# A table-driven order for PE, tight exp bursts, and half of the output products moved from VectorE to ScalarE and GpSimd, in an induced-attention and gated-FFN kernel

## The chip, the cores and the metric

One core of one Trainium2 chip. The metric is the time of one execution in microseconds (us) on the device; lower is better. Profiles come from one profiled execution; times come from further executions. The engines are called PE (TensorE matmul), PEld (weight load), DVE (VectorE), ACT (ScalarE), POOL (GpSimd) and SP (SyncE, which issues nearly all of the DMAs here).

## The reference, cut to what matters

```python
# x: (4, 12416, 128); inducing: (32, 128); d_ff = 1536
def mab(q, kv):                       # attention, one head
    s = scale * (q @ kv.transpose(0, 2, 1))
    a = softmax(s)
    return a @ kv
h = mab(I, x)                         # 32 inducing points look at all of x
y = mab(x, h)                         # every token looks at the 32 results
g, v = y @ w_gate, y @ w_val          # then per token:
ffn  = (gelu(g) * v) @ w_out
out  = y + sigmoid(y @ w_res) * ffn
```

Since y = a @ h with only 32 rows of h, the kernel folds h into the weights: the gate and value layers become products of 64 rows (two copies of the 32 attention weights, for precision) with `hgv = h @ w`, and two of them sit side by side in PE's 128 rows.

## The kernel before: the parts that matter

A batch is 24 groups of 512 tokens and one of 128. A group of 512 has six slots of 1024 columns (two blocks of 128 hidden values for each of the 512 tokens). Per slot PE makes two pairs of gate and value halves, ACT takes the gelu of each gate half, DVE multiplies (`u`), and PE later multiplies `u` with `wO` into the one bank `f`. In parallel the kernel prepares h for the next batch (exps "a", accumulation, exps "b").

```python
    p_ge  = ...tile_pool(name="gelu", bufs=7)
    p_u   = ...tile_pool(name="up", bufs=6)
    p_fin = ...tile_pool(name="fin", bufs=2)          # th and at: two buffers each
    ps_g  = ...(bufs=3, PSUM); ps_v = ...(bufs=2); ps_f = ...(bufs=1)
    # ...
    def emit(gate, value):          # one pair of halves
        # ... PE: g and v matmuls, 64 rows each
        act.activation(ge_t[i][...], gb, AC.Gelu, ...)               # ACT, f32
        ve.tensor_tensor(u, ge_t.pop(i), v_t.pop(i), AL.mult)        # DVE, per slot

    class Last:                     # the output of a group
        def gate(self):             # "R": tanh of the residual gate
            self.th = p_fin.tile([P, TOK], FP32, name="th", tag="th")
            act.activation(self.th, self.mix(slice(0, 64)), AC.Tanh, bias=0.0, scale=0.5)
        def residual(self):         # "A": y itself, copied out of PSUM
            self.at = p_fin.tile([P, TOK], FP32, name="at", tag="at")
            act.activation(self.at, self.mix(slice(64, 128)), AC.Copy, ...)
        def end(self):              # the output product, the sum, the store
            ve.scalar_tensor_tensor(th, th, 1.0, f, AL.add, AL.mult)
            po.tensor_tensor(at, at, th, AL.add)
            sy.dma_start(out[...], at)

    for gi in range(ngrp):          # the order: f is the group's first slot
        at(f + 2, lg.gate, START)
        for i, n in enumerate((16, 8, 6, 9, 9)):
            at(f + 3 + i, lambda lg=lg, n=n: lg.mms(n), END)         # 48 f matmuls
        at(f + 5, lg.residual, START)
        at(f + 7, lg.end, LATE)
    # ... exps of a batch in a burst with single slots between, without gelus;
    #     before it the lead of gelu halves grows by one a group, up to LEAD = 10
```

The softmax here doesn't subtract the row's maximum and nothing guards it: scores larger than these inputs give would overflow.

Of the kernel before, what the change touches and what calls it, by code (L numbers as in the profile page):

```python
# [18 lines left out]
def kernel(  # L19
# [34 lines left out]
    Q = 4  # L54
# [16 lines left out]
    p_ge = ctx.enter_context(tc.tile_pool(name="gelu", bufs=7))  # L71
    p_u = ctx.enter_context(tc.tile_pool(name="up", bufs=6))
# [71 lines left out]
    def exps(kind, b, j0, j1, bank):  # L144

        t0 = j0 // WIDE * WIDE
        if j0 == t0:
            dt = FP16 if kind == "a" else FP32
            if min(WIDE, nblk - t0) > 2:
                e_t[kind] = p_sm.tile([P, 2 * TOK], dt, name="e" + kind, tag="e" + kind, bufs=3)  # L150
            else:
                e_t[kind] = p_sm.tile([P, 2 * M], dt, name="es" + kind, tag="es" + kind, bufs=1)
# [200 lines left out]
    class Last:  # L353
# [41 lines left out]
        def end(self):  # L395
            tw = self.tw
            ve.scalar_tensor_tensor(self.th[:, :tw], self.th[:, :tw], 1.0,  # L397
                                    self.ffn.rearrange("p k c -> p (k c)")[:, :tw],
                                    AL.add, AL.mult)
            po.tensor_tensor(self.at[:, :tw], self.at[:, :tw], self.th[:, :tw], AL.add)  # L400
            n0, w = blocks_of(self.k)
            r0 = self.b * N + n0 * P
            sy.dma_start(
                out[r0:r0 + w * P, :].rearrange("(p j) c -> p j c", j=w)[
                    :, self.j0:self.j0 + self.nk, :],
                self.at[:, :tw].rearrange("p (k c) -> p k c", c=P))
# [94 lines left out]

    flat = [(gi, si) for gi in range(ngrp) for si in range(len(groups[gi][4]))]
    nflat = len(flat)
    first = {}
    for i, (gi, si) in enumerate(flat):
        first.setdefault(gi, i)
    windows = {}
    bursts = {}
    LEAD = 10

    START, MIDDLE, END, LATE = range(4)

    def at(i, f, where=MIDDLE):
        windows.setdefault(i, []).append((where, f))

    for gi in range(ngrp):
        lg = Last(gi)
        f = first[gi]
        at(f + 2, lg.gate, START)
        if len(groups[gi][4]) == 6:  # L520
            for i, n in enumerate((16, 8, 6, 9, 9)):
                at(f + 3 + i, lambda lg=lg, n=n: lg.mms(n), END)
            at(f + 5, lg.residual, START)
            at(f + 7, lg.end, LATE)
        else:
            at(f + 3, lg.residual, START)
            at(f + 3, lambda lg=lg: lg.mms(len(lg.todo)), END)
            at(f + 3, lg.end, LATE)

    def plan(b):  # L530
# [3 lines left out]
        def bg(g, p, f, where=MIDDLE):  # L534
            at(i0 + 6 * g + p, f, where)

        def burst(i, kind):
            n = TOK // M
            bursts[i] = [(lambda j0=j0: exps(kind, nb, j0, min(j0 + n, nblk), bank_g()))
                         for j0 in range(0, nblk, n)]  # L540

        if b == 0:
            for i in range(1, ntile):
                bg(0, 1 + (9 * i) // 2, lambda i=i: weights_b(0, i))
        if nb < B:
            for k in range(ntile):
                i = (9 * k) // 2 + 1
                bg(1, i, lambda k=k: fetch(nb, k))
                bg(1, i + 5, lambda k=k: convert(nb, k, po, po))
                bg(1, i + 8, lambda k=k: turn(nb, k))  # L550

            burst(i0 + 6 * 12 + 3, "a")
            cuts = [0, 20, 40, 60, 80, nblk]
            for i, (j0, j1) in enumerate(zip(cuts, cuts[1:])):
                bg(13 + i, 2, lambda j0=j0, j1=j1: accumulate(nb, j0, j1, True, True))
            bg(18, 2, lambda: finish_h(nb))
            bg(19, 2, lambda: turn_h(nb))
            bg(19, 4, lambda: first_layer_t(nb, 0))
            bg(20, 2, lambda: first_layer_t(nb, 1))
            bg(20, 4, lambda: spread(nb, 0, PRE))  # L560
            bg(20, 5, lambda: spread(nb, PRE, FCH))
            burst(i0 + 6 * 20 + 3, "b")
            tb = i0 + 6 * 21 + 3
            for i in range(0, nblk, WIDE):
                n = i // WIDE
                at(tb + 4 * n, lambda i=i: sums_b(nb, i, po))
                at(tb + 4 * n + 4, lambda i=i: ones_b(nb, i), LATE)
            bg(22, 2, lambda: res_layer(nb))
            for i in range(ntile):
                j = 6 * 21 + 9 + (5 * i) // 2  # L570
                at(i0 + j, lambda i=i: weights_b(nb, i), END)

    for b in range(B):
        plan(b)

    ghalves = [(i, h) for i in range(nflat) for h in range(len(halves_of(i)))]
    base = [0]
    for i in range(nflat):
        base.append(base[-1] + len(halves_of(i)))
    sent = {"g": 0, "v": 0, "w": 0}  # L580

    def slot(want):

        i = sent["v"]
        while sent["g"] < base[i + 1]:
            emit(ghalves[sent["g"]], None)
            sent["g"] += 1
        for h in range(len(halves_of(i))):
            g = None
            if sent["g"] < min(want, len(ghalves)):  # L590
                g = ghalves[sent["g"]]
# [66 lines left out]
```

## Time and profile before

| | before |
|---|---|
| time, median | 853.86 us (852.45, 852.99, 854.73; a fourth run of 2239.26 lies far off and counts as slow) |
| span of the profiled run (which took 849.61 us), mean granted clock of TensorE | 847.8 us, 0.985 |
| busy: PE, DVE, ACT, POOL | 94%, 92%, 89%, 45% |
| idle of ACT behind a buffer of `th` or `at` | 1.3 us in all |
| from the end of batch 0 to those of 1, 2 and 3 | 202.2, 203.7, 185.7 us |

The end of a batch is the start of its last group's output product, read from the timeline. The lines of this profile stand in the prediction below: the page's busy row, groups of instructions (busy time and mean of one, then the engine's idle time before them and what ended it), and busy times by stretch.

### The profile page before, as it was taken

To read this page: it belongs to the slowest core of one execution; us is meant where nothing else is said; L and a number is where in the kernel's file an instruction comes from. 1 tells how busy PE (TensorE), PEld (TensorE's weight loads), DVE (VectorE), ACT (ScalarE), POOL (GpSimd) and SP (SyncE) were. 2 spreads that over 40 slices of the span, in tenths; PEclk is the share of its full clock that TensorE was granted. 3 is DMA by queue.
4 is the path that set the end of the run, shared out by engine and by line. 5 is a ranking of instruction groups with operands and counts; after the bars stand their busy time and mean duration, and the time that the engine had idled before them with its cause. 6 is when DMAs were issued, how large, how long until landed. Compare 5 with 4: busy or idle time off the path is not lost.

```text
span 847.8 us, 23930 instructions
## 1 busy us (share of the span) xinstructions
PE 794.0 (94%) x9586; PEld 476.9 (56%) x9586; DVE 780.2 (92%) x773; ACT 757.8 (89%) x1462; POOL 381.2 (45%) x376
## 2 busy tenths in 40 slices
PE   5789999999999999999999999999999999999997
PEld 4545555555555555555655555555565555555554
DVE  8679999899799999899889999979979999999997
ACT  5589998899999999898999999979899999999994
POOL 2438985111498776112278878411229721111112
PEclk9699999999999999999999999999999999999999
DMA  8327874001247787100117888201022621100111
GB/s 299 125 68 163 205 194 121 26 27 39 45 95 156 178 196 146 41 27 31 52 39 118 200 183 185 73 27 39 27 56 68 121 57 39 39 36 30 38 39 43
DMA packets 118992, 78.28 MB, mean 92 GB/s; under 512 B 97216, under 2 KB 99936, under 8 KB 118880
## 3 DMA queue, kind: packets, MB, share of 16 engines
q1 hardware_dynamic: 116592, 74.32, 35.7%
q10 hardware_dynamic: 2288, 2.43, 0.9%
q8 instruction: 75, 1.23, 0.6%
q14 instruction: 37, 0.30, 0.1%
HBM read 27.87 MB, written 25.43 MB: 63 GB/s over the span
## 4 chain that ended last, share of the span: by engine, by line
PE 74%; ACT 16%; DVE 4%; issue 4%; DMA 1%; POOL 1%; POOLq 0%; SPq 0%; DVEq 0%; ACTq 0%
PE f L373 32%; PE g L336 31%; ACT ge L342 14%; PE v L336 4%; PE g L381 3%; PE g L157 2%; DVE lo L121 2%; DVE hi L119 1%; PE g L175 1%; ACT th L387 1%; PE g L177 1%; DVE u L350 0%; DMA xf<-in_x_dram 0%; DVE th L397 0%; POOL a L283 0%
## 5 line engine op out<-in xcount | busy, mean ns | idle before, releaser
L350 DVE TENSOR_TENSOR u<-ge,v 128x1024 bf16<-128x1024 f32 x584 | 690.0, 1213 | 51.8 <-ACT ge L342 23.5
L342 ACT ACTIVATE ge<-g 128x512 f32<-128x512 f32 x1164 | 621.0, 604 | 45.2 <-PE v L336 41.1
L336 PE MATMUL g<-rt,hgv 64*128 64x512 f16 x1152 | 370.0, 380 | 30.1 <-ACT ge L342 18.3
L336 PE MATMUL v<-rt,hgv 64*128 64x512 f16 x1152 | 381.8, 384 | 0.4 <-DVE u L350 0.2
L373 PE MATMUL f<-wO,u 128*128 128x128 bf16 x4656 | 345.1, 221 | 1.1 <-DVE th L397 1.1
L373 PEld LDWEIGHTS <-u 128*128 128x128 bf16 x4656 | 262.7, 98 | 116.1 <-issue 104.8
L400 POOL TENSOR_TENSOR at<-at,th 128x512 f32<-128x512 f32 (+1 forms) x100 | 124.2, 1242 | 392.5 <-ACT ge L342 355.9
L336 PEld LDWEIGHTS <-hgv 64*128 64x128 bf16 x2400 | 111.5, 94 | 158.9 <-issue 98.7
L283 POOL TENSOR_TENSOR a<-eb,z 128x1024 f16<-128x1024 f32 (+1 forms) x49 | 91.1, 1863 | 7.6 <-DMA rt<-a 5.8
L381 PEld LDWEIGHTS <-rt 64*128 64x128 f16 x768 | 56.5, 94 | 51.0 <-issue 16.9
L121 POOL TENSOR_TENSOR lo<-xf,hi 128x1024 f16<-128x1024 f32 x36 | 76.9, 2135 | 0.3
L381 PE MATMUL g<-hra,rt 64*128 64x128 f16 x768 | 73.5, 215 | 0.6
L397 DVE SCALAR_TENSOR_TENSOR th<-th,f 128x512 f32<-128x512 f32 (+1 forms) x100 | 66.5, 665 | 1.0 <-PE f L373 1.0
L387 ACT ACTIVATE th<-g 128x512 f32<-128x512 f32 (+1 forms) x100 | 59.5, 595 | 3.6 <-PE g L381 2.2
L392 ACT ACTIVATE at<-g 128x512 f32<-128x512 f32 (+1 forms) x100 | 59.4, 594 | 3.0 <-PE g L381 3.0
L119 POOL CAST hi<-xf 128x1024 f16<-128x1024 f32 x36 | 37.3, 1036 | 31.2 <-DMA xf<-in_x_dram 17.7
L157 PEld LDWEIGHTS <-xt 128*128 128x128 f16 x768 | 23.2, 98 | 12.0 <-issue 11.7
L137 ACT ACTIVATE xt<-g 128x1024 f16<-128x1024 f16 x12 | 12.3, 1023 | 13.5 <-PE g L136 13.5
L136 PE MATMUL g<-identF,hi 128*128 128x128 f16 x96 | 10.7, 279 | 10.0 <-DVE hi L119 9.9
L261 POOL TENSOR_TENSOR zt<-zt 128x256 f32<-128x256 f32 (+5 forms) x36 | 15.0, 417 | 2.8
L136 PEld LDWEIGHTS <-hi 128*128 128x128 f16 x96 | 8.0, 126 | 12.3 <-DVE hi L119 12.3
L161 ACT ACTIVATE eb<-g 128x512 f32<-128x512 f32 x18 | 10.1, 595 | 5.0 <-PE g L157 4.5
(104 smaller groups left out, 248.6 us busy)
## 6 DMA issues: line engine op xcount, KB each, us to landing
out_dram<-at SPq DMA_DIRECT2D x96, 256.0 KB, 2.2
xf<-in_x_dram SPq DMA_DIRECT2D x42, 512.0 KB, 4.1
ge<-in_x_dram SPq DMA_DIRECT2D x6, 512.0 KB, 5.9
rt<-a SPq DMA_TRANSPOSE x49, 3.1
xt<-hi SPq DMA_TRANSPOSE x36, 3.3
ge<-in_moe_w_gate_dram ACTq DMA_DIRECT2D x1, 512.0 KB, 4.6
ge<-in_moe_w_val_dram ACTq DMA_DIRECT2D x1, 512.0 KB, 5.0
ge<-in_moe_w_out_dram ACTq DMA_DIRECT2D x1, 512.0 KB, 4.4
```

The costliest lines, as they stand in the source:

```text
L119: e_hi.tensor_copy(hi[:, :w, :], xf[:, :w, :])
L121: e_lo.tensor_tensor(lo[:, :w, :P], xf[:, :w, :], hi[:, :w, :], AL.subtract)
L283: po.tensor_tensor(a2[:, :n], ev[:, o:o + n, :].unsqueeze(2).to_broadcast([P, n, Q, M]), z[:, o:o + n].unsqueeze(2).unsqueeze(3).to_broadc ...
L336: pe.matmul(*t[n], start=True, stop=True)
L342: act.activation(ge_t[i][:, h * TOK:h * TOK + n], gb[:, :n], AC.Gelu, bias=0.0, scale=1.0)
L350: ve.tensor_tensor(u[:, :n], ge_t.pop(i)[:, :n], v_t.pop(i)[:, :n], AL.mult)
L373: pe.matmul(self.ffn[:, k, :], u_t[self.gi, si][:, o:o + P], wO[:, fc, :], start=first, stop=not self.todo, skip_group_check=True)
L381: pe.matmul(bank[:, k * P:(k + 1) * P], rt_t[self.b, self.k][rows, self.j0 + k, :], hra_t[self.b][rows, :], start=True, stop=True)
L387: act.activation(self.th[:, :self.tw], self.mix(slice(0, 64)), AC.Tanh, bias=0.0, scale=0.5)
L392: act.activation(self.at[:, :self.tw], self.mix(slice(64, 128)), AC.Copy, bias=0.0, scale=1.0)
L397: ve.scalar_tensor_tensor(self.th[:, :tw], self.th[:, :tw], 1.0, self.ffn.rearrange("p k c -> p (k c)")[:, :tw], AL.add, AL.mult)
L400: po.tensor_tensor(self.at[:, :tw], self.at[:, :tw], self.th[:, :tw], AL.add)
```

## The change

The intent was to fill the waits between three almost full engines: PE's order of a batch comes from a table found with a model of the queues, the exps come in short bursts, and DVE is relieved of half of its output products.

In the table a word is one slot. P is a slot with two gate halves, Q with one, V with none, G a lone gate half; a number is so many f matmuls; R is a tanh, A a residual copy, E one burst piece of exps, c, h, t, l, r, o are steps of preparing h. A star marks a group whose output leaves by ACT and Pool.

```diff
-    p_ge = ...(name="gelu", bufs=7)
-    p_u  = ...(name="up", bufs=6)
+    p_ge = ...(name="gelu", bufs=8)
+    p_u  = ...(name="up", bufs=8)
     # ... exps "a" and "b" now share one set of buffers
-        def end(self):
-            ve.scalar_tensor_tensor(th, th, 1.0, f, AL.add, AL.mult)
-            po.tensor_tensor(at, at, th, AL.add)
+        def end(self, on_act):
+            if on_act:
+                fe = p_fin.tile([P, TOK], FP32, name="fe", tag="fe", bufs=1)
+                act.activation(fe, f, AC.Copy, bias=0.0, scale=1.0)
+                po.tensor_tensor(th, th, fe, AL.mult)
+                po.tensor_tensor(at, at, fe, AL.add)
+            else:
+                ve.scalar_tensor_tensor(th, th, 1.0, f, AL.add, AL.mult)
+            po.tensor_tensor(at, at, th, AL.add)
     # ...
+    plan = [
+        "ARQ GG6PRG 6P P8G P5 3P6",
+        "PR8G P2 7P A9P P8 GP *",
+        "9P A11P A9P 11P G12P 5P *",
     # ... 9 rows
+        "11P 10P R13P Q14E EVEc AEEE9EQ",
     # ... 12 rows
+    ]
     # ... the same without E, c, h, t, l, r, o for the last batch
+    LEAD = 4
     # ... the scheduled offsets of gate, mms, residual, end and the bursts are
     #     removed; the loop reads the words and sends what they name
```

More of the change, by code (lines that the diff above doesn't have):

```diff
@@ L70 @@
     p_h = ctx.enter_context(tc.tile_pool(name="hpool", bufs=2))
-    p_ge = ctx.enter_context(tc.tile_pool(name="gelu", bufs=7))
-    p_u = ctx.enter_context(tc.tile_pool(name="up", bufs=6))
+    p_ge = ctx.enter_context(tc.tile_pool(name="gelu", bufs=8))
+    p_u = ctx.enter_context(tc.tile_pool(name="up", bufs=8))
     p_fin = ctx.enter_context(tc.tile_pool(name="fin", bufs=2))
@@ L147, in exps @@
         if j0 == t0:
-            dt = FP16 if kind == "a" else FP32
             if min(WIDE, nblk - t0) > 2:
-                e_t[kind] = p_sm.tile([P, 2 * TOK], dt, name="e" + kind, tag="e" + kind, bufs=3)
+                e_t[kind] = p_sm.tile([P, 2 * TOK], FP32, name="e", tag="e", bufs=3)
             else:
-                e_t[kind] = p_sm.tile([P, 2 * M], dt, name="es" + kind, tag="es" + kind, bufs=1)
+                e_t[kind] = p_sm.tile([P, 2 * M], FP32, name="es", tag="es", bufs=1)
+            if kind == "a":
+                e_t[kind] = e_t[kind].bitcast(FP16)
         e = e_t[kind]
@@ L393, in residual @@
                            bias=0.0, scale=1.0)
-        def end(self):
+        def end(self, on_act):
             tw = self.tw
-            ve.scalar_tensor_tensor(self.th[:, :tw], self.th[:, :tw], 1.0,
-                                    self.ffn.rearrange("p k c -> p (k c)")[:, :tw],
-                                    AL.add, AL.mult)
-            po.tensor_tensor(self.at[:, :tw], self.at[:, :tw], self.th[:, :tw], AL.add)
+            th, at = self.th[:, :tw], self.at[:, :tw]
+            f = self.ffn.rearrange("p k c -> p (k c)")[:, :tw]
+            if on_act:
+                fe = p_fin.tile([P, TOK], FP32, name="fe", tag="fe", bufs=1)[:, :tw]
+                act.activation(fe, f, AC.Copy, bias=0.0, scale=1.0)
[4 more added lines that the diff above has]
+            po.tensor_tensor(at, at, th, AL.add)
             n0, w = blocks_of(self.k)
@@ L405, in end @@
                     :, self.j0:self.j0 + self.nk, :],
-                self.at[:, :tw].rearrange("p (k c) -> p k c", c=P))
+                at.rearrange("p (k c) -> p k c", c=P))
     ident = konst.tile([P, P], FP32, name="ident")
@@ L495 @@
         pe.matmul(warm, wG[:, :P], wG[:, :TOK], start=True, stop=True)
+    plan = [
+        "ARQ GG6PRG 6P P8G P5 3P6",
+        "PR8G P2 7P A9P P8 GP *",
+        "9P A11P A9P 11P G12P 5P *",
+        "7RQ R5P 7P 12GP 11P 7P",
+        "6P 6AP 9PG 9P P10 AP *",
+        "10PG 6P 9PR 13Q P 10RP",
+        "7PR 6P6 P9 PA10 PA P3 *",
+        "6P8 PA6 3P 7P 4P 11QR *",
+        "2P12 RP7 2P5 P 8P12 AP15A *",
+        "P9 P 5P6 2P11 RP 11P",
+        "8P5 P9 AP1 14P P12 RP",
+        "9P 6P 9PR9 3P P5 9AP",
+        "11P 10P R13P Q14E EVEc AEEE9EQ",
+        "P15 10P GcP6R P8 P5 P6",
+        "2P A8P 5PG8G AP8 P5 P6 *",
+        "3P A9P 6P 7PR1 3cP cP5 *",
+        "P9R P9 P2 3P8 P12 AP *",
+        "7cP 4P10 PR10 P5 hP 12PR *",
+        "12P 9PA 8P 7P 12P t11Q",
+        "AP11 AP 11P l6QRR 9Q AP9G",
+        "P6 3P 3P 16EEVEEE2EE 9Q P",
+        "24P5 P4 2P A7PR 6P P10 *",
+        "RP 12PoA 10P3 P13 rP11 PR *",
+        "10P4 P10 PR9l 4P Q 16P",
+        "8AP9o PG15oo",
+    ]
+    plan_last = [
+        "ARQ GG6PRG 6P P8G P5 3P6",
+        "PR8G P2 7P A9P P8 GP *",
+        "9P A11P A9P 11P G12P 5P *",
+        "7RQ R5P 7P 12GP 11P 7P",
+        "6P 6AP 9PG 9P P10 AP *",
+        "10PG 6P 9PR 13Q P 10RP",
+        "7PR 6P6 P9 PA10 PA P3 *",
+        "6P8 PA6 3P 7P 4P 11QR *",
+        "2P12 RP7 2P5 P 8P12 AP15A *",
+        "P9 P 5P6 2P11 RP 11P",
+        "8P5 P9 AP1 14P P12 RP",
+        "9P 6P 9PR9 3P P5 9AP",
+        "11P 10P R13P Q14 V A9Q",
+        "P15 10P GP6R P8 P5 P6",
+        "2P A8P 5PG8G AP8 P5 P6 *",
+        "3P A9P 6P 7PR1 3P P5 *",
+        "P9R P9 P2 3P8 P12 AP *",
+        "7P 4P10 PR10 P5 P 12PR *",
+        "12P 9PA 8P 7P 12P 11Q",
+        "AP11 AP 11P 6QRR 9Q AP9G",
+        "P6 3P 3P 16V2 9Q P",
+        "24P5 P4 2P A7PR 6P P10 *",
+        "RP 12PA 10P3 P13 P11 PR *",
+        "10P4 P10 PR9 4P Q 16P",
+        "8AP9 PG15",
+    ]
+    old = {"f": 12, "R": 1, "A": 1}
+    LEAD = 4
     flat = [(gi, si) for gi in range(ngrp) for si in range(len(groups[gi][4]))]
@@ L506 @@
         first.setdefault(gi, i)
+    ghalves = [(i, h) for i in range(nflat) for h in range(len(halves_of(i)))]
     windows = {}
-    bursts = {}
-    LEAD = 10
-    START, MIDDLE, END, LATE = range(4)
-    def at(i, f, where=MIDDLE):
-        windows.setdefault(i, []).append((where, f))
-    for gi in range(ngrp):
-        lg = Last(gi)
-        f = first[gi]
-        at(f + 2, lg.gate, START)
-        if len(groups[gi][4]) == 6:
-            for i, n in enumerate((16, 8, 6, 9, 9)):
-                at(f + 3 + i, lambda lg=lg, n=n: lg.mms(n), END)
-            at(f + 5, lg.residual, START)
-            at(f + 7, lg.end, LATE)
-        else:
-            at(f + 3, lg.residual, START)
-            at(f + 3, lambda lg=lg: lg.mms(len(lg.todo)), END)
-            at(f + 3, lg.end, LATE)
@@ L530, in plan, with plan_rest, at @@
-    def plan(b):
+    def plan_rest(b):
         nb = b + 1
         i0 = first[b * gpb]
-        def bg(g, p, f, where=MIDDLE):
-            at(i0 + 6 * g + p, f, where)
-        def burst(i, kind):
-            n = TOK // M
-            bursts[i] = [(lambda j0=j0: exps(kind, nb, j0, min(j0 + n, nblk), bank_g()))
-                         for j0 in range(0, nblk, n)]
+        def at(i, f):
+            windows.setdefault(i0 + i, []).append(f)
         if b == 0:
             for i in range(1, ntile):
-                bg(0, 1 + (9 * i) // 2, lambda i=i: weights_b(0, i))
+                at(1 + (9 * i) // 2, lambda i=i: weights_b(0, i))
@@ L545, in plan @@
         if nb < B:
             for k in range(ntile):
-                i = (9 * k) // 2 + 1
-                bg(1, i, lambda k=k: fetch(nb, k))
-                bg(1, i + 5, lambda k=k: convert(nb, k, po, po))
-                bg(1, i + 8, lambda k=k: turn(nb, k))
-            burst(i0 + 6 * 12 + 3, "a")
-            cuts = [0, 20, 40, 60, 80, nblk]
-            for i, (j0, j1) in enumerate(zip(cuts, cuts[1:])):
-                bg(13 + i, 2, lambda j0=j0, j1=j1: accumulate(nb, j0, j1, True, True))
@@ L556, in plan @@
-            bg(18, 2, lambda: finish_h(nb))
-            bg(19, 2, lambda: turn_h(nb))
-            bg(19, 4, lambda: first_layer_t(nb, 0))
-            bg(20, 2, lambda: first_layer_t(nb, 1))
-            bg(20, 4, lambda: spread(nb, 0, PRE))
-            bg(20, 5, lambda: spread(nb, PRE, FCH))
-            burst(i0 + 6 * 20 + 3, "b")
-            tb = i0 + 6 * 21 + 3
-            for i in range(0, nblk, WIDE):
-                n = i // WIDE
-                at(tb + 4 * n, lambda i=i: sums_b(nb, i, po))
-                at(tb + 4 * n + 4, lambda i=i: ones_b(nb, i), LATE)
@@ L568, in plan @@
-            bg(22, 2, lambda: res_layer(nb))
+                i = (9 * k) // 2 + 7
+                at(i, lambda k=k: fetch(nb, k))
+                at(i + 5, lambda k=k: convert(nb, k, po, po))
+                at(i + 8, lambda k=k: turn(nb, k))
             for i in range(ntile):
-                j = 6 * 21 + 9 + (5 * i) // 2
-                at(i0 + j, lambda i=i: weights_b(nb, i), END)
+                at(6 * 21 + 9 + (5 * i) // 2, lambda i=i: due.append((nb, i)))
     for b in range(B):
-        plan(b)
@@ L576 @@
-    ghalves = [(i, h) for i in range(nflat) for h in range(len(halves_of(i)))]
-    base = [0]
-    for i in range(nflat):
-        base.append(base[-1] + len(halves_of(i)))
-    sent = {"g": 0, "v": 0, "w": 0}
-    def slot(want):
-        i = sent["v"]
-        while sent["g"] < base[i + 1]:
-            emit(ghalves[sent["g"]], None)
-            sent["g"] += 1
-        for h in range(len(halves_of(i))):
-            g = None
-            if sent["g"] < min(want, len(ghalves)):
-                g = ghalves[sent["g"]]
-                sent["g"] += 1
-            emit(g, (i, h))
-        sent["v"] += 1
@@ L596, in window_next @@
-    def window_next():
-        for _, f in sorted(windows.pop(sent["w"], []), key=lambda e: e[0]):
-            f()
-        sent["w"] += 1
-    lead = 2
-    while sent["w"] < nflat:
-        i = sent["w"]
-        assert i == sent["v"]
-        if i in bursts:
-            pieces = bursts.pop(i)
-            n = 0
-            while pieces:
-                if sent["g"] >= base[sent["v"] + 1]:
-                    slot(0)
-                    for f in [pieces.pop(0) for _ in range(min(2 - n % 2, len(pieces)))]:
-                        f()
-                    window_next()
-                    n += 1
-                else:
-                    pieces.pop(0)()
-            lead = 2
-            continue
-        if flat[i][1] == 0 and len(groups[flat[i][0]][4]) == 6:
-            lead = min(lead + 1, LEAD)
-        want = base[i + 1] + lead
-        slot(want)
-        window_next()
-        if sent["g"] < min(want, len(ghalves)):
-            emit(ghalves[sent["g"]], None)
-            sent["g"] += 1
@@ L627, with single, gate_half @@
-    assert not bursts
-    while windows:
-        window_next()
+        plan_rest(b)
+    due = []
+    inverted = {}
+    lasts = []
+    sent = {"g": 0, "v": 0, "R": 0, "A": 0}
+    last_of = [Last(gi) for gi in range(ngrp)]
+    on_act = [row.endswith("*") for b in range(B) for row in (plan if b < B - 1 else plan_last)]
+    def single():
+        g = gate_half()
+        if g is not None:
+            emit(g, None)
+    def gate_half():
+        if sent["g"] == len(ghalves):
+            return None
+        sent["g"] += 1
+        return ghalves[sent["g"] - 1]
@@ new lines, in products_out, with background, step @@
+    def products_out(n):
+        while n and lasts:
+            lg = lasts[0]
+            k = min(n, len(lg.todo))
+            lg.mms(k)
+            n -= k
+            if not lg.todo:
+                lasts.pop(0).end(on_act[lg.gi])
+    def background(nb):
+        n = TOK // M
+        cuts = [0, 20, 40, 60, 80, nblk]
+        todo = {"E": [], "l": [], "c": [], "o": []}
+        for kind in "ab":
+            for j0 in range(0, nblk, n):
+                todo["E"].append((kind, j0, min(j0 + n, nblk)))
+        todo["c"] = list(zip(cuts, cuts[1:]))
+        todo["o"] = list(range(0, nblk, WIDE))
+        todo["l"] = [0, 1]
+        def step(t):
+            if t == "E":
+                kind, j0, j1 = todo["E"].pop(0)
+                exps(kind, nb, j0, j1, bank_g())
+                if kind == "b" and (j1 == nblk or j1 % WIDE == 0):
+                    sums_b(nb, j0 // WIDE * WIDE, po)
+            elif t == "c":
+                accumulate(nb, *todo["c"].pop(0), True, True)
+            elif t == "h":
+                finish_h(nb)
+            elif t == "t":
+                turn_h(nb)
+            elif t == "l":
+                first_layer_t(nb, todo["l"].pop(0))
+                if not todo["l"]:
+                    spread(nb, 0, PRE)
+                    spread(nb, PRE, FCH)
+            elif t == "r":
+                res_layer(nb)
+            elif t == "o":
+                t0 = todo["o"].pop(0)
+                ones_b(nb, t0)
+                inverted[nb] = t0 + WIDE
+        return step
@@ new lines @@
+    for _ in range(2):
+        single()
+    for b in range(B):
+        step = background(b + 1)
+        words = [w for row in (plan if b < B - 1 else plan_last) for w in row.replace(" *", "").split()]
+        for w in words:
+            i = sent["v"]
+            if flat[i][1] == 0:
+                lasts.append(last_of[flat[i][0]])
+            todo = []
+            for t in w:
+                if t.isdigit() and todo and todo[-1].isdigit():
+                    todo[-1] += t
+                else:
+                    todo.append(t)
+            for t in todo:
+                if t in "PQV":
+                    for h in range(len(halves_of(i))):
+                        emit(gate_half() if t == "P" or (t == "Q" and h == 0) else None, (i, h))
+                    sent["v"] += 1
+                elif t == "G":
+                    single()
+                elif t.isdigit():
+                    n = int(t)
+                    if b == 0:
+                        n -= min(old["f"], n)
+                        old["f"] -= int(t) - n
+                    products_out(n)
+                elif t in "RA":
+                    if b == 0 and old[t]:
+                        old[t] -= 1
+                    else:
+                        lg = last_of[sent[t]]
+                        sent[t] += 1
+                        lg.gate() if t == "R" else lg.residual()
+                else:
+                    step(t)
+            if b == 0 and i in range(4, 4 + 6 * (LEAD - 2), 6):
+                single()
+            for f in windows.pop(i, []):
+                f()
+            while due and (due[0][0], blocks_of(due[0][1])[0]) < (due[0][0], inverted.get(due[0][0], 0)):
+                weights_b(*due.pop(0))
@@ L631 @@
+    while sent["A"] < ngrp:
+        if sent["R"] < ngrp and sent["R"] <= sent["A"]:
+            last_of[sent["R"]].gate()
+            sent["R"] += 1
+        last_of[sent["A"]].residual()
+        sent["A"] += 1
+    while lasts:
+        products_out(48)
 _INS = ['x', 'inducing', 'moe_w_gate', 'moe_w_val', 'moe_w_out', 'moe_w_res']
```

## The prediction

> **What bounds the kernel now.** I read the page's busy row first, then the busy times by stretch, then the starts of instructions in the timeline, because three engines are nearly full and the mean cannot say which one sets the pace.
>
> The page's busy row and its costliest groups (busy, mean ns of one | idle before it):
>
> ```profile
> PE 794.0 (94%) x9586; PEld 476.9 (56%) x9586; DVE 780.2 (92%) x773; ACT 757.8 (89%) x1462; POOL 381.2 (45%) x376
> ...
> L350 DVE TENSOR_TENSOR u<-ge,v 128x1024 bf16<-128x1024 f32 x584 | 690.0, 1213 | 51.8 <-ACT ge L342 23.5
> L342 ACT ACTIVATE ge<-g 128x512 f32<-128x512 f32 x1164 | 621.0, 604 | 45.2 <-PE v L336 41.1
> L336 PE MATMUL g<-rt,hgv 64*128 64x512 f16 x1152 | 370.0, 380 | 30.1 <-ACT ge L342 18.3
> ...
> L397 DVE SCALAR_TENSOR_TENSOR th<-th,f 128x512 f32<-128x512 f32 (+1 forms) x100 | 66.5, 665 | 1.0 <-PE f L373 1.0
> ```
>
> No engine has long holes. PE waits for ACT, ACT for PE, DVE for ACT: a ring of small waits. The durations overlap their neighbours, so I take start-to-start times as cost. The timeline late in the run (start, length, engine, instructions):
>
> ```profile
> 721.53 0.68 DVE L397 SCALAR_TENSOR_TENSOR th<-th,f 128x512 f32<-128x512 f32 x1
> ...
> 722.13 7.10 DVE L350 TENSOR_TENSOR u<-ge,v 128x1024 bf16<-128x1024 f32 x6
> ...
> 722.70 1.07 PE L373 MATMUL f<-wO,u 128*128 128x128 bf16 x16
> ...
> 723.70 0.39 PE L336 MATMUL v<-rt,hgv 64*128 64x512 f16 x1
> ...
> 723.92 0.38 PE L336 MATMUL v<-rt,hgv 64*128 64x512 f16 x1
> ...
> 724.23 0.62 PE L373 MATMUL f<-wO,u 128*128 128x128 bf16 x8
> ...
> 726.18 0.60 ACT L392 ACTIVATE at<-g 128x512 f32<-128x512 f32 x1
> ...
> 726.65 3.28 ACT L342 ACTIVATE ge<-g 128x512 f32<-128x512 f32 x6
> ...
> 729.15 0.68 DVE L397 SCALAR_TENSOR_TENSOR th<-th,f 128x512 f32<-128x512 f32 x1
> ...
> 729.75 7.10 DVE L350 TENSOR_TENSOR u<-ge,v 128x1024 bf16<-128x1024 f32 x6
> ```
>
> A group (512 tokens, six slots) takes 729.75 - 722.13 = 7.62 us here, and DVE is never idle: six u products and one output product (th). The output product holds DVE for 729.75 - 729.15 = 0.60. An ACT instruction on one bank holds ACT for 726.65 - 726.18 = 0.47. Over all starts in the trace the shortest repeating distances are: u 1.138, gelu 0.485 (mean of two kinds), tanh or copy 0.477, table load 1.294. On PE a gate/value pair costs 0.222, an f matmul 0.056, a mix matmul 0.055, and going from pairs to f and back adds about 0.09 + 0.095 (0.31 instead of 0.22, 0.151 instead of 0.056).
>
> The stretches (us, then busy us of PE, PEld, DVE, ACT, POOL) show that the limit changes:
>
> ```profile
> 60.00:140.00 80.00, 76.86 (x820) 44.86 (x819) 76.87 (x72) 75.38 (x149) 70.14 (x60) 1.00 0.77 179
> 150.00:205.00 55.00, 53.20 (x726) 31.83 (x723) 49.26 (x51) 49.44 (x97) 8.36 (x8) 1.00 0.09 31
> 300.00:340.00 40.00, 37.95 (x418) 21.95 (x415) 39.66 (x38) 37.96 (x75) 28.52 (x28) 1.00 0.75 161
> 720.00:835.00 115.00, 109.88 (x1219) 64.16 (x1215) 113.97 (x107) 109.09 (x213) 19.14 (x15) 1.00 0.10 36
> ```
>
> The steady stretches (rows 3 and 4) are DVE's, at 99%, 7.61 us per group. Row 1 is where ACT makes an extra gelu half per group to rebuild the lead of ten halves: 7.94. Row 2 has the accumulation of h in blocks of 40 matmuls: 8.43, PE. The last output product of each batch starts at 252.7, 454.9, 658.5 and 844.2, so batches 1 and 2 take 202.2 and 203.7, while batch 3, which prepares no successor, takes 185.7. **Preparing the next batch costs 16.5 to 18**, about half of it in two exp bursts. In the second of batch 0 ACT makes no gelu from 216.14 to 224.40, 8.3 us, and the group there takes 11.7.
>
> **What the Trainium skill says.** "TensorEngine Tiling (Array Packing)", Key Properties: changing the tiling mode drains the TensorE. The trace agrees: the 64-row pairs and the 128-row f matmuls pay the 0.185 a round trip above. "ScalarE: Activation LUTs", What ACT_TABLE_LOAD costs: 1283 ns plus a drain of some 1380. The load is 1283 here, but the next instruction starts 1.294 after it, so I count no drain. "PSUM — Partial Sum Buffer", Specifications: GpSimd cannot access PSUM. That is why ACT must copy f before Pool can use it. "SBUF — State Buffer", SBUF: two separate sides: Pool blocks a DVE instruction with two SBUF inputs. The u product takes one input from PSUM, and it lasts 1218 ns with Pool 88% busy (60 to 110) and with Pool 17% busy (720 to 835), so more Pool work should not slow it.
>
> **The change part by part.**
> (1) Twelve of 25 groups per batch, 48 in all, send the output product by ACT and Pool. DVE loses 48 x 0.598 = 28.7. ACT gains 48 copies x 0.477 = 22.9. Pool gains 2 x 48 tensor operations of about 1.23 each, 118.
> (2) The order of PE. The built programs have the same matmuls. The runs of f grow from 484 to 526: 42 x 0.185 = +7.8 on PE.
> (3) Exps in tight bursts: seven exps and two loads make 6 x 0.49 + 0.25 + 2 x 1.294 = 5.8 of ACT instead of the 8.3 seen. Table loads are not fewer. Six bursts x 2.5 = -15 at most.
> (4) Accumulation no longer sits as a block behind a slot, and the lead is 4 halves instead of 10, so no groups of thirteen gelu halves. Buffers for ge and u grow by one and two.
>
> Demand of the main loop (all after about 45 us), which now takes 798:
> - DVE before: 580 x 1.138 + 96 x 0.598 + 8 small = 725. After: 696.
> - ACT before: 1164 x 0.485 + 192 x 0.477 + 36 exps x 0.49 + 12 loads x 1.294 + 7 = 697. After: 720.
> - PE after: f 4656 x 0.056 = 261; pairs 1057 x 0.222 + 48 short = 237; lone gates and values 190 x 0.222 = 42; mixes 776 x 0.055 = 43; exps 582 x 0.025 = 15; accumulation 8; switches 526 x 0.185 + 5 = 102: 708. Before: 700.
>
> So the largest demand barely falls (725 to 720). **The move of products balances; the gain must come from the 73 us of holes that the order leaves.** A steady group after asks DVE for 6 x 1.138 + 0.3 = 7.13, ACT for 12 x 0.485 + 2.5 x 0.477 = 7.01, and PE for about 6.98 (708 less 34 for preparing, over 97). Before, DVE asked 7.43 and the group took 7.61, 2.4% more. I put 3% on 7.13, since three engines now lie close: 7.35. A batch is 24.25 groups: 178 instead of 185.7. Preparing asks ACT for some 13 (exps 6.4, loads 5.2, rest 1.3) and PE for about 12, partly side by side: I take 13, so batches 1 and 2 take 191 each.
>
> Batch 0 differs, because Pool also makes most of the weights of its own batch. From the built order, between its first and its last marked end in the first ten groups, Pool does 12 converts x 3.2 = 38.5, ten weights x 1.85 = 18.5 and 22 output operations x 1.23 = 27: 84, where ten groups at 7.35 are 74. Two buffers of th and of at can hide a lag of a group or so. I add 5: 196.
>
> Sum: 50 before the first batch's groups + 196 + 191 + 191 + 178 + 3.6 tail = 810, plus 6 (timed 854.73 against a span of 847.8) = 816. A table found in a model is not fully met on a chip; I add 4: **820 us**, 4% less.
>
> **Rivals.**
> - Pool takes DVE's place. One fe buffer and two of th and at tie ACT to Pool, and PE to ACT. For it: row 1 above, Pool at 88% already. Against: from 150 to 205 Pool is 15% busy, and batches 1 to 3 make fewer weights there. If it holds over a dozen groups in each of three batches, 8.2 per group: 840.
> - ACT becomes the bound. 720 of demand in a loop of 760 is 95%, and every late gate bank stops PE. Then groups stay at 7.5 to 7.6 and only the bursts and the rebuilding of the lead gain, 5 to 7 a batch: 832.
> - The short lead starves DVE in a burst: 4 halves are two u, 2.3 us against 5.8 without gelu. It is in the 13 above; if two bursts cost as now, 828.
> - The order is met exactly and PE's 708 is the limit: loop 740 to 745, so 800.
>
> **Range and chances.** The rivals span 800 to 840, so 800 to 842 holds 8 in 10. 2% faster is 837.6, above all rivals but one. Faster 0.78, same 0.18, slower 0.04.
>
> **What would show it.** DVE's th group x52 instead of x100, a new ACT group fe<-f x48 near 600 ns, three Pool operations per marked group. Ends of batches about 191 apart and the last 178; steady groups 7.2 to 7.45, none at 7.94 or 8.43; stretches without gelu near 6 instead of 8.3. Batch 0 slowest, Pool near full from 55 to 135. Wrong if ACT waits for Pool (fe, th) for tens of us, if DVE waits at bursts for more than 3 us each, or if u gets longer beside Pool.

## The result, and the profile after

The changed kernel takes **977.99 us** (974.61 to 979.63, four runs), against 853.86. The ratio is 1.1455, 95% interval 1.1409 to 1.1501: 14.6% slower. Ratios here and below are the mean time of one kernel's fast runs over that of the other's of the same rounds, so not quite the ratio of the medians quoted. The result is correct.

The page of the changed kernel, the busy row and the groups that answer to those of before:

```profile
PE 827.8 (85%) x9585; PEld 495.8 (51%) x9586; DVE 754.8 (77%) x725; ACT 773.7 (79%) x1510; POOL 500.3 (51%) x472
...
L351 DVE TENSOR_TENSOR u<-ge,v 128x1024 bf16<-128x1024 f32 x584 | 685.5, 1214 | 175.6 <-PE v L337 89.7
...
L337 PE MATMUL g<-rt,hgv 64*128 64x512 f16 x1152 | 392.1, 403 | 102.9 <-ACT at L393 66.2
...
L393 ACT ACTIVATE at<-g 128x512 f32<-128x512 f32 (+1 forms) x100 | 58.9, 589 | 104.0 <-DMA out_dram<-at 98.4
```

DVE has lost its 48 products (x725 instead of x773), as intended, but it now idles 175.6 us ahead of the u products instead of 51.8. The new name is in the last row: ACT idles 98.4 us ahead of the residual copy, and an output DMA ends it. PE's gate matmuls in turn wait 66.2 us for that copy. The list of waits of ACT (who waited, for whom: total us, times, longest):

```profile
ACT at L393 <- DMA out_dram<-at: 98.4, 28, 7.1
...
ACT th L388 <- POOL at L407: 19.8, 9, 6.5
```

In the kernel before there is no wait of the first kind, and one of the second:

```profile
ACT th L387 <- POOL at L400: 1.3, 1, 1.3
```

One such wait of the changed kernel (start, length, engine, instructions, idle before and what ended it), put together from the timelines of DVE, Pool, ACT, SP and ACT again:

```profile
239.38 0.69 DVE L406 SCALAR_TENSOR_TENSOR th<-th,f 128x512 f32<-128x512 f32 x1 [1.49 <-PE f L374]
...
237.63 1.28 POOL L259 TENSOR_TENSOR zt<-e 128x512 f32<-128x512 f32 x1 [10.83 <-ACT e L162]
...
249.07 1.26 POOL L407 TENSOR_TENSOR at<-at,th 128x512 f32<-128x512 f32 x1
...
240.92 4.51 ACT L343 ACTIVATE ge<-g 128x512 f32<-128x512 f32 x9
...
250.36 0.33 SPq L410 DMA_DIRECT2D out_dram<-at  x1
...
252.47 0.60 ACT L393 ACTIVATE at<-g 128x512 f32<-128x512 f32 x1 [7.04 <-DMA out_dram<-at]
```

Group 21's residual copy stands next in ACT's queue at 245.4. It needs the buffer of group 19, whose product was made at 239.4. But Pool first works off the sums of the exps "b", put into its queue earlier, adds group 19's residual only at 249.07, and SP sends the store at 250.36. ACT starts at 252.47, 7 us late, and the gelus behind it are late with it. Group 21 waits as long in batches 1 and 2 (7.1 us each). The stretch around it (us, busy us of PE, PEld, DVE, ACT, POOL, then the granted clock):

```profile
240.00:260.00 20.00, 12.68 (x124) 7.53 (x122) 11.53 (x12) 11.62 (x23) 10.27 (x20) 0.74 0.07 27
```

PE, DVE, ACT and Pool are busy only 51 to 63% of it, and the granted clock falls to 0.74; over the whole run it is 0.916 against 0.985. The Trainium skill, "TensorE: Matmul & The Clock Gate", HAM oscillation, warns of PE-idle gaps over some 3.4 us, after which the clock is throttled. The trace agrees in kind: after a 6.25 us idle of PE at 100.52, its gate matmuls last 0.58 to 0.61 us there, against 0.37 to 0.39 just before.

### The profile page after: what moved, and what is told of

The parts are those of the page before. It is cut to its first block, busy times and chain, and to the rows that moved or that the text cites. A ratio compares the mean times of both kernels' runs of the same rounds, so it can differ in the third digit from the quotient of the medians.

```text
span 975.1 us, 23933 instructions
## 1 busy us (share of the span) xinstructions
PE 827.8 (85%) x9585; PEld 495.8 (51%) x9586; DVE 754.8 (77%) x725; ACT 773.7 (79%) x1510; POOL 500.3 (51%) x472
## 5 line engine op out<-in xcount | busy, mean ns | idle before, releaser
L351 DVE TENSOR_TENSOR u<-ge,v 128x1024 bf16<-128x1024 f32 x584 | 685.5, 1214 | 175.6 <-PE v L337 89.7
L343 ACT ACTIVATE ge<-g 128x512 f32<-128x512 f32 x1164 | 607.6, 617 | 44.2 <-PE v L337 24.5
L337 PE MATMUL g<-rt,hgv 64*128 64x512 f16 x1152 | 392.1, 403 | 102.9 <-ACT at L393 66.2
L374 PE MATMUL f<-wO,u 128*128 128x128 bf16 x4656 | 370.8, 227 | 2.0 <-ACT fe L402 1.0
L374 PEld LDWEIGHTS <-u 128*128 128x128 bf16 x4656 | 279.2, 101 | 149.0 <-issue 138.1
L337 PEld LDWEIGHTS <-hgv 64*128 64x128 bf16 x2400 | 127.0, 95 | 230.7 <-issue 163.2
L393 ACT ACTIVATE at<-g 128x512 f32<-128x512 f32 (+1 forms) x100 | 58.9, 589 | 104.0 <-DMA out_dram<-at 98.4
L403 POOL TENSOR_TENSOR th<-th,fe 128x512 f32<-128x512 f32 x48 | 61.2, 1276 | 151.9 <-ACT fe L402 130.8
L284 POOL TENSOR_TENSOR a<-e,z 128x1024 f16<-128x1024 f32 (+1 forms) x49 | 90.9, 1863 | 11.3 <-DMA rt<-a 5.2
L388 ACT ACTIVATE th<-g 128x512 f32<-128x512 f32 (+1 forms) x100 | 59.5, 599 | 25.2 <-POOL at L407 19.8
L404 POOL TENSOR_TENSOR at<-at,fe 128x512 f32<-128x512 f32 x48 | 61.2, 1274 | 0.0
L406 DVE SCALAR_TENSOR_TENSOR th<-th,f 128x512 f32<-128x512 f32 (+1 forms) x52 | 33.9, 652 | 30.3 <-ACT th L388 22.3
L402 ACT ACTIVATE fe<-f 128x512 f32<-128x512 f32 x48 | 29.5, 615 | 5.3 <-PE f L374 4.6
L259 POOL TENSOR_TENSOR zt<-e 128x512 f32<-128x512 f32 x9 | 11.6, 1284 | 33.5 <-ACT e L162 33.0
```

The lines of the kernel that those rows point to most:

```text
L284: po.tensor_tensor(a2[:, :n], ev[:, o:o + n, :].unsqueeze(2).to_broadcast([P, n, Q, M]), z[:, o:o + n].unsqueeze(2).unsqueeze(3).to_broadc ...
L337: pe.matmul(*t[n], start=True, stop=True)
L343: act.activation(ge_t[i][:, h * TOK:h * TOK + n], gb[:, :n], AC.Gelu, bias=0.0, scale=1.0)
L351: ve.tensor_tensor(u[:, :n], ge_t.pop(i)[:, :n], v_t.pop(i)[:, :n], AL.mult)
L374: pe.matmul(self.ffn[:, k, :], u_t[self.gi, si][:, o:o + P], wO[:, fc, :], start=first, stop=not self.todo, skip_group_check=True)
L388: act.activation(self.th[:, :self.tw], self.mix(slice(0, 64)), AC.Tanh, bias=0.0, scale=0.5)
```

## The experiments

**Theory T (turnaround).** The table sends many R and A too soon. Counted from it, a residual copy comes 1 to 13 slots after the end of the group two before (1 in groups 9 and 20, 3 in group 19, 4 in groups 7, 10, 15 and 22), where the kernel before left 10 (5 to 9 next to the short group of 128; for `th` it is seven slots). ACT runs its queue in order, so it stands behind a buffer that Pool and the output DMA still hold. (The count is not the whole of it. Of the 28 waits, 12 are those of groups 9, 19 and 20 in each of the four batches, but group 22, four slots after, never waits and group 15 once, while group 21, five slots after, waits longest. What Pool has in its queue before that buffer counts too, as above.) **Theory P:** the three Pool operations of a marked group are too slow whatever the order. **Theory L:** the short lead of gelu halves starves DVE at the bursts.

### e1_defer: the same table, R and A held back

```diff
-                        lg.gate() if t == "R" else lg.residual()
+                        held.append((t, sent[t]))
+                        release()
     # ... release() sends what is held 7 slots after the end of the group two before,
     #     or when its own group is to end
```

> The changed kernel (978 us), its table and its routes kept; only a tanh or a residual copy is sent to the engines no sooner than seven slots after the group two before it has ended, so that its buffer of th or at is free when ACT comes to it. Theory T (turnaround: the table sends them one to five slots after that end, ACT stands in its queue behind a buffer that Pool and the output DMA still hold, and PE and DVE stand behind ACT): the 98 us of at <- DMA and 20 us of th <- Pool fall under 20 us together, time 850 to 890. Theory P (three Pool operations per marked group are too slow whatever the order): time stays above 940. Theory L (lead of four halves and tight bursts starve DVE): time stays above 930, waits of ACT gone.

889.8 us (ratio 1.0479). The waits of ACT for `at` fell to 27.7 us, those for `th` to 3.5:

```profile
ACT at L393 <- DMA out_dram<-at: 27.7, 13, 4.2
```

The waits are not all gone: together they are 31 us, where T expected under 20, and the time is at the upper end of what T gave. Nine of the 13 waits for `at` (15 us) come behind a marked group. The other four (12.5 us) come behind an unmarked one, and three of them are group 21 again, behind Pool's sums of the exps. Sending R and A later, with nothing else changed, takes back some 88 of the 124 us lost.

### e2_fin3: a third buffer of th and of at

```diff
-            self.th = p_fin.tile([P, TOK], FP32, name="th", tag="th")
+            self.th = p_fin.tile([P, TOK], FP32, name="th", tag="th", bufs=3)
-            self.at = p_fin.tile([P, TOK], FP32, name="at", tag="at")
+            self.at = p_fin.tile([P, TOK], FP32, name="at", tag="at", bufs=3)
-    p_ge = ...(name="gelu", bufs=8)
+    p_ge = ...(name="gelu", bufs=7)     # for the room
```

> The changed kernel with three buffers of th and of at instead of two (one buffer of ge given up for the room, 7 instead of 8). Order and routes the same. Theory T: the waits of ACT for the output DMA and for Pool nearly vanish, time 840 to 890. Theory P: Pool's chain of three operations still delays, time above 940. Theory L: above 930.

856.39 us (ratio 1.0086): nearly all of the loss is gone with one more buffer each, as T expected. The granted clock is 0.971, and ACT's wait for the output DMA is down from 98.4 us to:

```profile
ACT at L393 <- DMA out_dram<-at: 8.2, 5, 1.9
```

### e9_ge7 and e10_at3: which of the three edits did it

```diff
 e9_ge7:   ge bufs 8 -> 7, th and at stay at two
 e10_at3:  ge bufs 8 -> 7, at gets three buffers, th stays at two
```

> Control for the run with three buffers of th and at (856), which also gave up one of the eight ge buffers: the changed kernel with seven ge buffers and nothing else. If the third th and at buffers made the 122 us of difference: no better than the changed kernel, 975 to 990. If the eighth ge buffer did harm: clearly below 970.

> The changed kernel with seven ge buffers and a third buffer of at alone; th keeps two. The waits of ACT were 98 us for at (released by the output DMA) and 20 us for th (released by Pool). If the residual's buffer is the one: the 98 us go and the time is 860 to 895, with the waits for th at 20 us or somewhat more. If th matters as much: over 910.

e9_ge7 took 979.74 us, the same as the changed kernel: the ge buffer has no part in it. e10_at3 took 875.75 us. So the third `at` is worth 979.7 - 875.8 = 104 us, and the third `th`, from there to 856.4, another 19. With `at` mended, ACT stands behind `th` more than it did (32.0 us instead of 19.8):

```profile
ACT th L388 <- POOL at L407: 32.0, 19, 6.0
```

### e3_no_act: every product back on DVE, two buffers

```diff
-                lasts.pop(0).end(on_act[lg.gi])
+                lasts.pop(0).end(False)
```

> The changed kernel with the order kept, but every output product on DVE again, none by ACT and Pool. Theory P: the whole loss goes, 840 to 870. Theory T: the release of th and at comes some 2.5 us earlier in marked groups, the waits in unmarked groups stay (A one slot after the end), so a third to a half of the loss goes: 900 to 940. Theory L: 960 or more.

924.93 us (ratio 1.0893), inside what T gave and outside P and L. A product on DVE frees `at` after one Pool operation instead of three, which shortens the waits (67.3 us of ACT for the DMA instead of 98.4) but doesn't remove them: the order is enough to make them.

### e4_before_early: the same fault put into the kernel before

```diff
-            at(f + 5, lg.residual, START)
+            at(max(f - 4, 0), lg.residual, LATE if gi > 1 else START)
```

> The kernel before (854 us) with one thing changed: the residual copy is sent one slot after the group two before it has ended, nine slots sooner than it was. If theory T is right this alone breaks the good kernel: ACT waits 1.3 (Pool) + 2 (DMA) + issue, some 2 to 3 us per group, for the output DMA, 100 to 250 us of waits in all and a time of 950 to 1050, with a lower granted clock. If ACT's waits are hidden by the lead of ten gelu halves, it stays within 3% of 854.

**1162.19 us** (ratio 1.3687). One line of order, with no other engine, buffer or product changed, costs 313 us (the kernel before took 849.22). The list of waits has the same pair as the changed kernel, in 90 of 100 groups:

```profile
ACT at L392 <- DMA out_dram<-at: 277.4, 90, 5.1
...
PE g L336 <- ACT at L392: 171.8, 86, 4.2
```

I expected 100 to 250 us of waits and 950 to 1050. The waits came out a little above that (277.4 us), and their price well above: each wait of 3.1 us on ACT costs the loop some 3.5 us, the lower clock (0.906) included. The lead of up to ten gelu halves did not hide it.

### e5_fin3_no_act, e6_fin3_late, e11_fin3_last: what the move to ACT and Pool is worth

With three buffers, so that the turnaround no longer hides it, the marks (all marked groups in e2_fin3) were removed altogether, in the first thirteen groups of batches 0 to 2, and everywhere but in the last batch.

```diff
 e5_fin3_no_act:  end(False) for all groups
 e6_fin3_late:    marked only where b == B - 1 or the row is past the 13th
 e11_fin3_last:   marked only where b == B - 1
```

> Three buffers of th and at (which gave 856), and in addition every output product on DVE again. Tells what the move to ACT and Pool is worth once the buffers do not stop ACT. If Pool, overloaded by the move in the first half of batches 0 to 2, is what keeps the 856 from the 820 predicted: it falls, to 835 to 848. If the move balances the engines as predicted: DVE gets 29 us more and the time rises to 865 to 880.

> Three buffers of th and at; products leave by ACT and Pool only where Pool has room (the second half of batches 0 to 2, and the whole last batch). If Pool's load in the first half is the rest of the loss: batch 0 falls from 210 to about 200 and batches 1 and 2 by some 4 each, 836 to 845. If the rest lies in the order itself (bursts, short lead, groups over 8 us without background): within 5 us of 856.

> Three buffers of th and at, and products by ACT and Pool in the last batch only, where Pool has nothing else to do. Put together from the batches of the two runs with three buffers: batches 0 to 2 as with all products on DVE (start to 654.3), the last as with the move (183.1): a span of 841 and a time of 840 to 844, the best of both.

| kernel | time | ratio | from first product to end of batch 0 | batch 1 | batch 2 | batch 3 |
|---|---|---|---|---|---|---|
| before | 853.9 | 1 | 195.4 | 202.2 | 203.7 | 185.7 |
| after | 978.0 | 1.1455 | 233.4 | 237.3 | 238.9 | 204.7 |
| e2_fin3, all marks | 856.4 | 1.0086 | 201.1 | 206.6 | 201.7 | 183.1 |
| e5_fin3_no_act, no marks | 848.0 | 0.9935 | 193.5 | 200.2 | 199.9 | 188.6 |
| e6_fin3_late | 845.8 | 0.9912 | 194.7 | 201.3 | 203.0 | 183.1 |
| e11_fin3_last | **843.7** | **0.9885** | 195.5 | 200.3 | 199.9 | 182.9 |

The move gains 188.6 - 183.1 = 5.5 us in the last batch, where Pool has nothing else to do. It costs 7.6 us in batch 0, where Pool makes the weights and converts the next batch: ACT stands there once for 7.3 us (at 122.4 in e2_fin3), until Pool has read the one buffer of `fe`. In batches 1 and 2 it costs 6.4 and 1.8 us. e5_fin3_no_act (848.0) is at the upper edge of what Pool's load gave and far from the 865 to 880 of a move that balances; e6_fin3_late (845.8) missed its 836 to 845 by under 1 us, e11_fin3_last met its own. The version with marks in the last batch only, put together from these columns before it ran, is the best correct kernel: 1.15% faster than the kernel before (95% interval 0.7 to 1.6%).

### e12_lead6: a longer lead

```diff
-    LEAD = 4
+    LEAD = 6            # on e11_fin3_last
```

> The kernel of e11_fin3_last with two more gelu halves made ahead of use during the first batch and kept from there on (lead six instead of four). Theory L, that the short lead starves DVE at the exp bursts: DVE's idle time in the 16 us from a burst's start falls from 3.2 and 2.8 to under 2 and the time by 4 to 10 us. If PE's order and its waits are the limit instead: within 3 us of that kernel.

925.68 us, 82 us more than e11_fin3_last, which neither theory expected. DVE's idle time in the 16 us from a burst's start did not fall (3.23 and 2.79 us in e11_fin3_last, 4.01 and 2.78 here). In the kernel before, with its long lead, it was 3.5 and 4.1, so the short lead starves DVE at the bursts no more than the old order did. The list of waits names the cause of the longer time (the same wait is 5.3 us in e11_fin3_last):

```profile
ACT ge L343 <- DVE u L351: 74.8, 123, 1.9
```

It is the same fault with another buffer: two more gelu halves need one more ge tile, there are only seven, and ACT stands in its queue until DVE has read one. So this run says nothing against a longer lead with enough buffers; that stays open. It is one more case of an order and a number of buffers that don't fit.

### e7_before_act, e8_before_act_late: the move alone, in the old order

```diff
 e7: end(on_act) as in the change, for groups 1, 2, 4, 6, 7, 8, 14 to 17, 21, 22 of every batch
 e8: the same for groups 12, 14, 16, 18 of batches 0 to 2, and for thirteen of the last batch
```

> The kernel before (849 to 854) with its own order and its two buffers, only the same twelve of 25 groups' products sent by ACT and Pool. There ACT comes to a buffer some 10 us after Pool has done with it, so theory T expects no waits of ACT for at or th beyond 10 us in all. If the move alone is worth anything: the steady DVE-bound groups fall from 7.61 to about 7.3 in the last batch, but Pool is overloaded in the first half of batch 0: 842 to 856. If Pool's three operations harm by themselves: over 865.

> The kernel before with products sent by ACT and Pool only where Pool has room: four groups in the second half of batches 0 to 2, and thirteen of the last batch. The last batch should go from 185.7 to 178 to 181, the others stay: 840 to 848, the best so far if the move is worth anything. If PE, not DVE, sets the pace of the steady groups, no change: within 2 us of the kernel before.

891.29 us (1.0441) and 871.03 us (1.02, 95% interval 1.015 to 1.025): both slower. e7 lies in the branch that Pool's three operations do harm by themselves (over 865), e8 outside both of its own. T's part held roughly: the waits for `th` and `at` in e7 are 11.0 and 2.4 us, a little over the 10 expected, and 4.5 more are for `fe`. What failed is the gain itself. In the last batch of e8, marked and unmarked groups alternate, and two take 7.14 + 8.41 = 15.55 us instead of 2 x 7.61 = 15.22. The timeline there shows why:

```profile
796.38 0.60 ACT L401 ACTIVATE fe<-f 128x512 f32<-128x512 f32 x1
...
796.86 1.11 ACT L342 ACTIVATE ge<-g 128x512 f32<-128x512 f32 x2
...
797.53 0.37 PE L336 MATMUL g<-rt,hgv 64*128 64x512 f16 x1 [0.57 <-ACT ge L342]
...
797.82 0.64 ACT L387 ACTIVATE th<-g 128x512 f32<-128x512 f32 x1
...
798.52 1.22 DVE L350 TENSOR_TENSOR u<-ge,v 128x1024 bf16<-128x1024 f32 x1 [0.43 <-ACT th L387]
```

The copy of f holds ACT for half a microsecond just where PE needs a gelu bank back. PE's wait there grows from 0.25 to 0.57 us, and the DVE that has been relieved waits. This fits the last batch of e8, which takes 3.9 us more than before, but not all of the loss: of the 23 us between the two profiled runs 12.8 lie in batch 0, where ACT waits twice for `th`, 7.4 us in all, before any marked group has ended. Why it waits there is not known. Nor is Pool's share in the loss of e7 parted from that of the copy.

### e13_before_no_th, e14_fin3_no_th: is DVE the bound at all?

The product (tanh + 1) x f is left out. Their outputs are wrong, which doesn't matter for the times. (The comparison with the reference still passed both, as the term is small for these inputs; the kernels are not valid all the same.)

```diff
-            ve.scalar_tensor_tensor(th, th, 1.0, f, AL.add, AL.mult)
+            # nothing; at + th goes out
```

> WRONG RESULTS ON PURPOSE. The kernel before with its output product (tanh + 1) x f left out: DVE loses 100 instructions, 0.598 us each, 60 us of demand, and no engine gets anything in exchange. The prediction took the steady groups (7.61 us, DVE 99% busy) as set by DVE. If they are: these groups fall to about 7.0 and the time to 815 to 830. If the order of PE and ACT sets them and DVE only fills the same time: groups stay within 0.15 of 7.61 and the time within 12 us of the kernel before.

> WRONG RESULTS ON PURPOSE. The same product left out of the kernel with the new order, three buffers of th and at and all products on DVE (848). If DVE bounds it: 800 to 820. If PE's order and its waits for gelu banks bound it: 835 or more, which leaves the move of products to ACT and Pool nothing to win in either order.

In the old order, 60 us of DVE work taken away for nothing gave 847.11 us, ratio 0.9934 (0.9900 to 0.9969). The steady groups still take 7.61 us. The same stretch of the kernel before and of e13_before_no_th (first PE, PEld, DVE, ACT, POOL), one fence each:

```profile
720.00:810.00 90.00, 85.91 (x949) 49.94 (x946) 89.25 (x84) 85.27 (x167) 15.31 (x12) 1.00 0.10 37
```

```profile
720.00:810.00 90.00, 85.91 (x950) 49.97 (x947) 83.89 (x71) 85.28 (x166) 15.36 (x12) 1.00 0.10 37
```

PE's 85.91 and ACT's 85.27 don't move; only DVE's 89.25 becomes 83.89. **The engine that was busy 99% did not set the pace.** What is left to set it is the order of PE and ACT, by elimination, and DVE just fitted in.

In the new order the same removal gives 818.00 us, against 847.96 for e5_fin3_no_act (each against the kernel before: ratios 0.9603 and 0.9935). There DVE's product does stand in the way. In e5_fin3_no_act PE waits 26.5 us, in 41 places, for a product to free the single f bank, where the kernel before waits 1.1 us:

```profile
PE f L374 <- DVE th L406: 26.5, 41, 1.0
```

So the new order is faster by about 30 us if the product costs nothing, and no route tried here makes it cost nothing.

## Why the prediction was wrong, point by point

- **"The largest demand barely falls; the gain must come from the holes that the order leaves."** The main sums were right: the costs hardly changed (u 1213 to 1214 ns on the mean, gelu 604 to 617, f 221 to 227), and the order, freed of its product, does reach 818. But the prediction treated the holes as something a table fills. The changed table opened larger ones. (Two slips in the sums decide nothing: 708 less 34 over 97 groups is 6.95, not 6.98, and the 6 us added to the span pairs two executions. The profiled one took 849.61 us at a span of 847.8, 1.8 apart.)
- **The step that failed** is "Two buffers of th and of at can hide a lag of a group or so. I add 5". It weighed Pool's load against Pool's time and never counted how many slots lie between the release of a buffer and its next use. That number stood in the table (1 to 13, against 10 before) and in the built order, before any run. Measured: 104 us for `at` and 19 for `th`. The prediction named the symptom to look for ("wrong if ACT waits for Pool (fe, th) for tens of us"), and its first rival had the tie of ACT to Pool, but it sized it at 20 us in all and thought of Pool's speed, not of the order. The largest wait was not among those it named: for the store of `at`.
- **"Steady stretches are DVE's, at 99%"**, and from it 7.35 us for a steady group after. e13_before_no_th shows this false for the kernel before. The skill's "Perfetto Trace Analysis", Identifying the Most-Contended Engine, points to the engine of highest occupancy; in the old order it was the wrong one. In the new order, with the buffers mended, groups are not even either: in the last batch of e2_fin3 they take 6.3 to 10.2 us up to the last two, and the batch 183.1, not the 178 foreseen.
- **Part 1, the move.** Its counts were right (DVE x725, fe x48). Its worth was not: 5.5 us in the last batch of the new order instead of the 7.7 (185.7 to 178) predicted for that batch as a whole, a loss in the others, and a loss everywhere in the old order.
- **Batch 0 and Pool.** The 84 us of Pool work against 74, worth 5 us, was sound once the buffers were out of the way: the marks cost 7.6 us there (201.1 against 193.5).
- **Part 3, the bursts,** was right. From the last gelu before a burst to the first after it (start to start) it was 9.76 and 9.75 us before, and is 7.20 and 6.38 in e11_fin3_last. Three times 2.6 and 3.4 us make 18, near the 15 foreseen. Preparing the next batch costs 11.6 and 11.3 us in e5_fin3_no_act (200.2 and 199.9 less 188.6), against 16.5 and 18.0 before and 13 foreseen.
- **DVE unharmed by Pool** was right: u lasts 1213 ns on the mean before and 1214 after.
- What stays open: how much of the loss is the lower granted clock. It rises with the waits gone (0.916, 0.971 in e2_fin3, 0.983 in e11_fin3_last), and no run parts it from them.

## What to carry to other kernels

When an order of issue is changed, count for every buffer how long after its release it is taken again, through all engines and DMAs that hold it, before looking at any engine's load: an engine that runs its queue in order stops for everyone behind it. A third buffer, or a later place in the queue, is the cheap remedy, and both should be tried before a new order is judged. And before moving work off the busiest engine, take that work away for nothing in a trial run, in the order that you mean to use: if the time stays, as it did in the old order here, the engine was only keeping pace; in the new order the same trial gave 30 us.

## What the Trainium skill lacked or had wrong

- "Perfetto Trace Analysis", Identifying the Most-Contended Engine: it says of Vector that occupancy is a fair measure of how close it is to its roofline, and to optimize the engine of highest occupancy first. DVE was 99% busy in the steady stretch (89.25 of 90 us), and 60 us less work for it changed the time by 0.7%.
- The same page, Optimization Strategy, says that consistent bubbles, the same gap repeating for a stretch, can mean too few buffers. The runs agree, with a size that it lacks: one buffer more of a 128x512 f32 tile was worth 104 us of 980. But the bubbles did not repeat along a stretch: they fell on 28 of 100 groups, mostly the same six to eight of each batch, and were up to 7.1 us long. It does not say that moving the use alone does the same harm (849 to 1162 us).
- "ScalarE: Activation LUTs", What ACT_TABLE_LOAD costs: the drain of some 1380 ns after a load is not seen; the next instruction starts 1.294 us after the load starts, at every one of the 13 loads of the kernel before and at 12 of 13 of the changed one.
- "TensorEngine Tiling (Array Packing)", Key Properties: it says that a change of mode drains, with no figure. Here it was about 0.09 us from 64-row pairs to 128-row matmuls and 0.095 back.
